# Block B's q and k for tokens 0 to 1023: seven block products for eight, in turns with plain groups

## The chip, the cores and the metric

The kernel runs on one core of one Trainium2 chip. The metric is device time in microseconds of one execution; the times are medians of several runs. The engines are named as in the profile: PE (TensorE matmul) with PEld (its weight load), DVE (VectorE), ACT (ScalarE), POOL (GpSimd) and SP (SyncE, which here issues nearly all DMAs, in the order in which they were written). Every engine works its instructions off in program order.

## What is computed

Two attention blocks on independent inputs of 2048 tokens x 640, their outputs side by side. Block A is local and dilated (8 keys, 2 apart), block B full attention; both have 32 heads of 20. All is float32.

```python
# block A: per token 8 keys, idx = pos - 2 * (0..7)
qkv = x @ wqkv ; logits = q . k[idx] * Dh**-0.5 ; o = softmax(logits) . v[idx] ; out_a = o @ wo
# block B
qkv = x @ wqkv ; p = softmax(q k^T * Dh**-0.5) ; out_b = (p v) @ wo
return concatenate([out_a, out_b], -1)
```

A float32 operand is kept as two parts, `hi` (rounded to the type that PE multiplies at full rate) and `lo = x - hi`; a product of two operands is three matmuls, hi·hi, hi·lo and lo·hi (`PASSES`). Contraction over 640 is five chunks of 128 (`KC`), so a plain output tile of 128 x 512 is 15 matmuls.

## The kernel before

The program is one long function, `attention_pair`, in four stages; nearly every instruction is issued through a recording helper, so the profile gives them one line (L61) and they are told apart by tile names.

1. Block A's q, k and v for most tokens (`a_steps`, to about 148 us). Much of it is in quads (`a_quad`): four output tiles by seven block products with sums of operands (Strassen's method in Winograd's form) in place of eight, with a fifth chunk added plainly. Results go to `qa_d`, `ka_d`, `va_d` in DRAM.
2. Block B's q and k (148 to 284 us), the stage that the change rewrites.
3. Block B's v (28 groups of 15 matmuls with 320 columns, `v_group`), and from its eighth group on the first maxima (`b_max`) of block B's scores.
4. Block B's scores, exponentials and products with v, a hand-written order of PE's work over some 1300 us, with block A's attention on POOL beside it, then the output products.

Stage 2 before is one loop (`for m in range(0, 10, 2)`): five pairs of weight blocks (`WB`, 128 q or k features each, in the order `MS`), for each four token tiles of 512 (`XB[n]`, tile names `xn` for chunks 0 to 3 and `xl` for chunk 4) and for each the two blocks: 40 groups. A group is 15 matmuls into one PSUM bank, ACT copies the high part to an output tile `pr`, DVE subtracts for the low part, and SP stores both (512 KB) to `qb_d` or `kb_d`. The output tiles come from the ring `p` of `PB` = 6 buffers. The next pair of weights is loaded through the ring `stg`, and split by ACT and DVE, two groups after the loop has reached the second token tile.

`tick()` counts groups; `after(n, fn)` places a step n ticks later, so the numbers of groups set the program order. `a_work` is the generator `a_attention`: each `next(a_work)` gives POOL one unit of block A's attention (two keys or two values of 128 tokens; tiles `akv`, with queries in `aq`), and lets SP fetch the unit after the next one (`a_fetch(n + 2)`) into a ring of 4 `akv` buffers. In stage 2 it is called after 12 of the groups 5 to 33. Four `ve` tiles, set to one by POOL before the stage, wait for stage 3 (the ones give block B's softmax sums).

In the last four groups SP also loads the keys of the first four heads (`bk`, from `kb_d`), then in stage 3 the queries (`bq`, from `qb_d`); the first maxima need both.

## Time and profile before

| | us |
|---|---|
| median of 3 runs (lowest to highest) | 1742.59 (1742.42 to 1743.18) |
| the profiled execution | 1743.04 |
| its span in the profile | 1741.3 |
| PE busy | 1728.7 (99%) |
| stage 2, first matmul to stage 3's first | 147.91 to 284.31 |
| stage 3's first maxima matmul | 300.71 |

How to read it: "busy" is the time in which an engine had an instruction at work; matmuls are pipelined, so the time that one matmul costs is read from the distance of starts and not from its duration (a row's mean of 389 ns holds two in flight). A row of a timeline gives start, duration, engine, line, operation and tiles (out<-in), a count of merged instructions, and in brackets the idle time before it with what ended it. The profile lacks some matmul records (their counts in short windows are a few per cent low). "SPq" is SP's queue; the clock column is the granted PE clock, 1.00 in every window shown.

### The profile page before, as it was taken

The page shows a single profiled execution, that of the slowest core. Times are in us where ns is not written, and L with a number is a line of the kernel's source. Part 1 is how long each engine was busy: PE and PEld are TensorE (multiplying, and loading weights), DVE is VectorE, ACT ScalarE, POOL GpSimd, SP SyncE. Part 2 cuts the span into 40 slices and gives each one's busy share as a digit, 9 for nine tenths or more (in the row PEclk, how much of TensorE's full clock was granted, in tenths as well). Part 3 has the DMA queues.
Part 4 walks back from the last instruction along what each step waited for, and adds up shares of the span by engine and source line. Part 5 has one row for each costly group of instructions (what it writes and reads, how often), then busy time and mean ns, then how long its engine had stood idle before and what let it go on. Part 6 is the DMA issues. An engine that isn't in the chain of part 4 may idle for free.

```text
span 1741.3 us, 32202 instructions
## 1 busy us (share of the span) xinstructions
PE 1728.7 (99%) x11223; PEld 981.1 (56%) x11223; DVE 1466.4 (84%) x2062; ACT 1335.5 (77%) x2603; POOL 1248.2 (72%) x1138
## 2 busy tenths in 40 slices
PE   9999999999999999999999999999999999999999
PEld 8888888874444444444444444444444444444558
DVE  7756232789999999999999999999999999999656
ACT  5224222239999999999999999999999999998882
POOL 0000991786888888887998898988888898768324
PEclk9999999999999999999999999999999999999999
DMA  7668877864546544644465455536552634231223
GB/s 236 216 215 302 289 271 239 251 194 122 165 126 145 149 132 133 168 147 139 138 171 150 133 149 142 166 104 176 147 153 91 156 100 141 67 104 47 65 74 117
DMA packets 224411, 271.20 MB, mean 156 GB/s; under 512 B 92908, under 2 KB 147448, under 8 KB 224248
## 3 DMA queue, kind: packets, MB, share of 16 engines
q1 hardware_dynamic: 223672, 268.49, 52.4%
q8 instruction: 88, 1.44, 0.4%
q14 instruction: 75, 0.61, 0.1%
q10 hardware_dynamic: 576, 0.66, 0.1%
HBM read 194.31 MB, written 74.74 MB: 155 GB/s over the span
## 4 chain that ended last, share of the span: by engine, by line
PE 94%; DVE 2%; ACT 1%; DMA 1%; issue 1%; SPq 0%; POOL 0%; DVEq 0%; POOLq 0%; ACTq 0%
PE ps_st L61 94%; DVE mx L61 2%; ACT e L61 1%; DMA bk<-kb_d 1%; DMA vb_d<-ve 0%; ACT more L61 0%; DMA qb_d<-pr 0%; DVE mtr L61 0%; SPq L61 0%; POOL am L61 0%; DVE ro L61 0%; DVE pr L61 0%; ACT al L61 0%; ACT pr L61 0%; ACT braw L61 0%
## 5 line engine op out<-in xcount | busy, mean ns | idle before, releaser
L61 DVE TENSOR_REDUCE mx<-ps_st 128x1 f32<-128x512 f32 (+1 forms) x1500 | 1217.7, 877 | 76.5 <-PE ps_st L61 65.5
L61 ACT ACTIVATE e<-ps_st 128x512 f32<-128x512 f32 x2048 | 1067.4, 609 | 45.2 <-PE ps_st L61 25.8
L61 PE MATMUL ps_st<-bq,bk 62*128 62x512 f32 x2048 | 612.8, 439 | 0.2
L61 PE MATMUL ps_st<-bk,bq 60*128 60x512 f32 x2048 | 557.5, 435 | 2.6 <-DVE mx L61 0.9
L61 PEld LDWEIGHTS ps_st<-bq,bk 62*128 62x128 f32 x2048 | 287.4, 184 | 481.0 <-ACT e L61 337.3
L61 PE MATMUL ps_st<-e,vb 128*32 128x512 f32 x4096 | 542.9, 604 | 2.1
L61 POOL TENSOR_TENSOR braw<-braw,more 128x512 f32<-128x512 f32 x224 | 287.8, 1285 | 124.4 <-ACT more L61 116.2
L61 POOL TENSOR_TENSOR akv<-akv 128x640 f32<-128x640 f32 (+3 forms) x304 | 282.2, 928 | 23.8
L61 PEld LDWEIGHTS ps_st<-bk,bq 60*128 60x128 f32 x2048 | 265.4, 184 | 35.8 <-DVE mx L61 11.9
L61 POOL TENSOR_TENSOR akv<-akv,aq 128x1280 f32<-128x1280 f32 x64 | 188.8, 2950 | 21.9 <-DMA akv<-ka_d 21.8
L61 PEld LDWEIGHTS ps_st<-e,vb 128*32 128x32 f32 x4096 | 82.0, 108 | 156.1 <-issue 70.8
L61 POOL TENSOR_TENSOR akv<-akv,al 128x1280 f32<-128x1280 f32 x64 | 152.0, 2375 | 0.2
L61 ACT COPY more<-ps_st 128x512 f32<-128x512 f32 x224 | 132.5, 591 | 1.9 <-PE ps_st L61 1.0
L61 PE MATMUL ps_st<-wc,xn 128*128 128x512 f32 (+1 forms) x544 | 133.7, 378 | 0.0
L61 ACT COPY ro<-ps_st 128x320 f32<-128x320 f32 (+2 forms) x76 | 34.8, 460 | 106.2 <-PE ps_st L61 85.1
L61 PE MATMUL ps_st<-xn,w 128*128 128x512 f32 x480 | 115.4, 389 | 0.0
L61 PEld LDWEIGHTS ps_st<-wc,xn 128*128 128x128 f32 x544 | 102.4, 188 | 14.7
L61 POOL MEMSET ve<- 128x347 f32 x4 | 1.4, 390 | 148.5 <-DVE ro L61 137.2
L61 PEld LDWEIGHTS ps_st<-xn,w 128*128 128x128 f32 x480 | 90.0, 188 | 18.9 <-issue 0.2
L61 DVE TENSOR_TENSOR pr<-ps_st,pr 128x512 fp32r<-128x512 f32 x40 | 27.6, 690 | 84.8 <-ACT pr L61 84.8
L61 ACT CAST pr<-ps_st 128x512 fp32r<-128x512 f32 x40 | 23.5, 588 | 97.2 <-PE ps_st L61 92.8
L61 PE MATMUL ps_st<-ww,aot 128*128 128x320 f32 x480 | 77.8, 314 | 1.7
(109 smaller groups left out, 1325.6 us busy)
## 6 DMA issues: line engine op xcount, KB each, us to landing
akv<-ka_d SPq DMA_DIRECT2D x128, 320.0 KB
akv<-va_d SPq DMA_DIRECT2D x128, 320.0 KB
wx<-wa_d SPq DMA_DIRECT2D x24, 480.0 KB
kb_d<-pr SPq DMA_DIRECT2D x20, 512.0 KB
qb_d<-pr SPq DMA_DIRECT2D x20, 512.0 KB
bk<-kb_d SPq DMA_DIRECT2D x16, 640.0 KB
bq<-qb_d SPq DMA_DIRECT2D x64, 160.0 KB
rb<-s_d SPq DMA_DIRECT2D x128, 64.0 KB
```

Of the source, the lines that this page charges most:

```text
L61: return self.tc.keep_in_program_order(op(*a, **k))
```

## The change

In stage 2 the eight tiles of a weight pair by four token tiles are parted. Token tiles 2 and 3 stay plain (`b_plain`: four groups of 15). Token tiles 0 and 1 with the pair's two weight blocks become a four (`b_four`): the weight blocks' even and odd chunks are A11, A12 (first block) and A21, A22 (second), the token tiles' are B11, B21 and B12, B22; sums S1 to S4 of the former and T1 to T4 of the latter make seven products of 2 chunks x 3 passes, and the fifth chunk is added to each of the four results. A four is parted at four places (30, 6, 15 and 3 matmuls), and each counts as a group. The turns are: plain 0, plain 1, four 0, four 1, plain 2, four 2, plain 3, four 3, four 4, plain 4.

- The token sums (`XFour`, tiles `xs`, `xn`) are made once, by POOL on the raw tiles after groups 2 and 4; their parts by ACT and DVE (`base`, `second`). The weight sums (`WFour`) are made on POOL for pairs 0 and 1 and on DVE for pairs 2 to 4, and parted likewise. `jobs` says after which group each stands; pair 1's weights are loaded after group 0.
- Partial results are summed by DVE (tiles `sum` in the rings `raw` and `rb`). The low part of an output and its store stand one group later (`low`).
- The ring `p` of 6 becomes two rings `px` and `p` of 3, taken in turns elsewhere; in stage 2 all outputs use the 3 of `p` and `px` holds parts of the tokens. The ring `akv` becomes `akv` and `akx` of 2 each; in stage 2 (`narrow`) the attention units have only the 2 of `akv`, their first fetches stand at groups 7 and 9, and the fetch of unit n + 2 stands three groups after unit n. The units stand at groups 9 to 33, again 12.
- The `ve` tiles are set to one at the end of the stage. Large tiles change places (`big` 0 and 1 with 2 and 3), since the plain tiles are now 2 and 3; `ident` moves into the ring `am`.

```diff
+    def p_tile(shape, dt=F32R, name="wc", tag=None):
+
+        if tag is None:
+            turn_p[0] += 1
+            tag = ("px", "p")[turn_p[0] % 2]
+        return sb.tile(shape, dt, tag=tag, bufs=PB // 2, name=name)
...
-        kv = sb.tile([128, 2, D], F32, tag="akv", bufs=4, name="akv")
+        turn_kv[0] += not narrow[0]
+        kv = sb.tile([128, 2, D], F32, tag=("akv", "akx")[turn_kv[0] % 2], bufs=2, name="akv")
...
-            a_fetch(n + 2)
+            if not narrow[0]:
+                a_fetch(n + 2)
...
+            if narrow[0]:
+                after(3, a_fetch, n + 2)
...
+        def sums(self, kp):
+            a, b = self.raw[kp]
+            pool(b[:, 1], b[:, 1], b[:, 0], ALU.subtract)
+            pool(b[:, 0], b[:, 0], a[:, 0], ALU.subtract)
+            pool(a[:, 0], b[:, 1], a[:, 0], ALU.add)
+            pool(a[:, 1], a[:, 1], a[:, 0], ALU.subtract)
+
+        def second(self, kp):
+            u, e = self.u[1][:, :, 2 * kp:2 * kp + 2], self.e[kp]
+            self.parts(u[:, 0], u[:, 1], self.raw[kp][0])
+            for n in range(2):
+                self.parts(e[n + 1][:, 0], e[n + 1][:, 1], self.raw[kp][1][:, n])
...
-    groups = 0
-    for m in range(0, 10, 2):
-        nxt = []
-        for n in range(4):
-            for j in range(2):
-                p = next(banks)
-                for k in range(KC):
-                    for i, (wi, xi) in enumerate(PASSES):
-                        pe.matmul(p, WB[j][:, wi, k], chunk(XB[n], xi, k), start=(k == 0 and i == 0),
-                                  stop=(k == KC - 1 and i == 2))
...
-                pt = sb.tile([128, 2, 512], F32R, tag="p", bufs=PB, name="pr")
-                act.copy(pt[:, o[0]], p)
-                dve.tensor_tensor(pt[:, o[1]], p, pt[:, o[0]].bitcast(F32), ALU.subtract)
-                after(1, sp.dma_start, dst_b(c, n).rearrange("t p c -> p t c"), pt.bitcast(F32))
-                tick()
...
+    def b_parts(p, c, n, first=None, wait=False):
+
+        o = (0, 1) if c < KC else (1, 0)
+        pt = p_tile([128, 2, 512], F32R, "pr", "p")
+        src = p
+        if first is not None:
+            src = pt[:, o[1]].bitcast(F32)
+            add(src, first, p)
+        if wait:
+            lows.append(lambda: act.copy(pt[:, o[0]], src))
+        else:
+            act.copy(pt[:, o[0]], src)
+
+        def lo():
+            lo_of(pt[:, o[1]], src, pt[:, o[0]])
+            sp.dma_start(dst_b(c, n).rearrange("t p c -> p t c"), pt.bitcast(F32))
+        lows.append(lo)
...
+        product(b[0], A11, B11, True, True)
+        act.copy(c[0], b[0])
+        low()
+        product(b[3], w.S(4) + v1, B22 + l2, True, True)
+        product(b[1], w.S(2), x.T(2), True, True)
+        add(c[1], c[0], b[1])
+        product(b[0], A12 + v1, B21 + l1, False, True)
+        b_parts(b[0], m[0], 0)
+        yield
+        product(b[2], w.S(1), x.T(1), True, True)
+        add(c[1], c[1], b[2])
+        low()
+        b_parts(b[3], m[0], 1, c[1])
+        yield
+        product(b[1], w.S(3), x.T(3), False, True)
+        add(c[0], c[0], b[1])
+        low()
+        product(b[4], A22 + v2, x.T(4) + l1, True, True)
+        b_parts(b[4], m[1], 0, c[0])
+        yield
+        product(b[2], v2, l2, False, True)
+        b_parts(b[2], m[1], 1, c[0], True)
+        low(2)
+        yield
...
+    jobs = {0: (kp1, lambda: WF.append(WFour(1, "stg", 3))), 1: (lambda: XW.base(0),),
+            2: (lambda: XW.sums(0), lambda: WF[1].base()), 3: (lambda: WF[0].sums(gp), lambda: XW.ends([ends_x[1][:, o] for o in range(2)])),
+            4: (lambda: XW.second(0), lambda: XW.base(1), lambda: XW.sums(1)), 5: (lambda: WF[0].second(), lambda: WF[1].sums(gp)),
+            6: (lambda: XW.second(1),), 7: (lambda: a_fetch(0),), 8: (lambda: WF[1].second(),), 9: (lambda: a_fetch(1),)}
+    for m, at in ((2, (10, 13, 16, 18)), (3, (18, 21, 24, 25)), (4, (25, 27, 28, 29))):
...
+        if groups in (9, 11, 14, 16, 18, 21, 23, 25, 27, 29, 31, 33):
+            next(a_work, None)
```

How this moves the instructions is seen on three engines. On PE, where plain groups of before become the fourth four (`xn`, `xl`, `xs`: token tiles; `w`: weights):

```order
-L61 MATMUL ps_st<-xn,w 128x512 x12
+L61 MATMUL ps_st<-xn,w 128x512 x6
+L61 MATMUL ps_st<-xs,w 128x512 x6
 L61 MATMUL ps_st<-xl,w 128x512 x3
 L61 MATMUL ps_st<-xn,w 128x512 x12
 L61 MATMUL ps_st<-xl,w 128x512 x3
-L61 MATMUL ps_st<-xn,w 128x512 x12
+L61 MATMUL ps_st<-xs,w 128x512 x12
+L61 MATMUL ps_st<-xn,w 128x512 x6
+L61 MATMUL ps_st<-xl,w 128x512 x6
```

The rows with + or a blank are one four: 6 + 6 + 3 + 12 + 3 + 12 + 6 + 6 = 54 matmuls, where four plain groups have 60.

On POOL, at the start of its work in stage 2, before (`ve`: the tiles set to one; `akv`: the first attention unit):

```order
L61 MEMSET zero 7x128
L61 MEMSET ve 128x347 x4
L61 TENSOR_TENSOR akv<-akv,aq 128x1280
L61 TENSOR_TENSOR akv<-akv 128x2x320
L61 TENSOR_TENSOR akv<-akv 128x2x160
```

and now (`stg`: raw tokens, 512 wide, and raw weights, 2x128):

```order
L61 MEMSET zero 7x128
L61 TENSOR_TENSOR stg<-stg 128x512 x4
L61 TENSOR_TENSOR stg<-stg 128x2x128 x4
L61 TENSOR_TENSOR stg<-stg 128x512 x4
L61 TENSOR_TENSOR stg<-stg 128x2x128 x4
L61 TENSOR_TENSOR akv<-akv,aq 128x1280
```

Sixteen sums stand ahead of the first unit, and the four settings have gone behind the last one.

On SP's queue, at the end of stage 2, before (`pr`: outputs; `wv_b`: weights of stage 3; `bk`: keys for the maxima):

```order
L61 DMA stg<-wv_b 128x320
L61 DMA bk<-kb_d 40x4x1024
L61 DMA qb_d<-pr 128x2x512
L61 DMA bk<-kb_d 22x4x1024
L61 DMA qb_d<-pr 128x2x512
L61 DMA stg<-wv_b 128x640 x2
L61 DMA stg<-wv_b 128x320
L61 DMA bk<-kb_d 40x4x1024
L61 DMA qb_d<-pr 128x2x512
L61 DMA bk<-kb_d 22x4x1024
L61 DMA vb_d<-ve 128x336
```

and now (`akv`: the fetch of an attention unit's keys):

```order
L61 DMA akv<-ka_d 128x640 x2
L61 DMA stg<-wv_b 128x320
L61 DMA bk<-kb_d 40x4x1024
L61 DMA qb_d<-pr 128x2x512
L61 DMA bk<-kb_d 22x4x1024
L61 DMA qb_d<-pr 128x2x512
L61 DMA stg<-wv_b 128x640 x2
L61 DMA stg<-wv_b 128x320
L61 DMA bk<-kb_d 40x4x1024
L61 DMA qb_d<-pr 128x2x512
L61 DMA bk<-kb_d 22x4x1024
L61 DMA qb_d<-pr 128x2x512
```

A key fetch has come in ahead of the key loads, and each `bk` load now stands one store earlier: the last of them ahead of the last group's store, which `vb_d<-ve` follows.

More of the change, by code (lines that the diff above doesn't have):

```diff
@@ L299, in __init__ @@
                 w = [sb.tile([128, 3, n], F32R, tag="w", bufs=4, name="wc") for _ in range(4)]
-                p = [sb.tile([128, 2, n], F32R, tag="p", bufs=PB, name="wc") for _ in range(PB)]
+                p = [p_tile([128, 2, n]) for _ in range(PB)]
                 self.b11 = [[w[2 * kp + i][:, 2] for i in range(2)] for kp in range(2)]
@@ L313, in __init__ @@
             self.c = [[lambda i, j=j: self.last[j][i]] for j in range(2)]
-            self.raw = [sb.tile([128, 2, n], F32, tag=tag, bufs=2 * (P + 1), name="wr") for tag, _ in self.tags for _ in range(2)]
+            self.raw = [sb.tile([128, 2, n], F32, tag=tag, bufs=2, name="wr") for tag, _ in self.tags for _ in range(2)]
             self.raw.append(end)
@@ L700, in x_raw @@
+    XW, WF = XFour(), []
     def x_raw(n, a, b, tag, bufs):
@@ L834, in attention_pair @@
[L834 removed]
+                t = 3 - o if n == 44 else o
+                sp.dma_start(r[:, o], xb[(KC - 1) * 128:, t * 512:(t + 1) * 512])
+            ends_x.append(r)
         if n == 45:
[L836 to L840 removed]
+            WF[0].base()
         elif n == 46:
[L842 removed]
@@ L843, in attention_pair @@
-            x_parts(0, KC - 1, ends_x[0])
+            XB[3][1] = sb.tile([128, 2, 1, 512], F32R, tag="last1", bufs=2, name="xl")
+            x_parts(3, KC - 1, ends_x[0][:, :1])
         if n in (45, 46):
-            raw_x += [x_raw(n - 43, a, b, "p", PB) for a, b in PAIRS[:2]]
-    XB.append(columns(1))
-    x_parts(1, 0, raw_x[0])
-    x_parts(1, 2, raw_x[1])
-    x_parts(1, KC - 1, ends_x[1])
+            a, b = PAIRS[n - 45]
+            r = p_tile([128, b - a, 512], F32, "stg", "p")
+            sp.dma_start(r, xb[a * 128:b * 128, 1024:1536].rearrange("(k p) c -> p k c", p=128))
@@ L850, in attention_pair @@
+            raw_x.append(r)
+    XB[2] = columns(2)
+    x_parts(2, 0, raw_x[2])
+    x_parts(2, 2, raw_x[3])
+    x_parts(2, KC - 1, ends_x[0][:, 1:])
     assert not keeps
-    ones = [sb.tile([128, 16 * VC + 11], F32, tag=tag, bufs=2, name="ve") for tag in ("raw", "rb", "raw", "rb")]
-    for t in ones:
-        gp.memset(t, 1.0)
     wait[0] = 2
@@ new lines, in b_four @@
+    def b_four(w, x):
+        A11, A12, A22 = ([w.block(j, 2 * kp + o) for kp in range(2)] for j, o in ((0, 0), (0, 1), (1, 1)))
+        B11, B21, B22 = ([f(kp) for kp in range(2)] for f in (x.B11, x.B21, x.B22))
+        v1, v2 = ([w.block(j, KC - 1)] for j in range(2))
+        l1, l2 = ([t] for t in x.l)
+        m = w.m
+        b = [next_bank() for _ in range(5)]
+        c = [sb.tile([128, 512], F32, tag=tag, bufs=2, name="sum") for tag in ("raw", "rb")]
+        product(b[0], A11, B11, True, True)
[22 more added lines that the diff above has]
+        yield
@@ new lines, in b_plain, with groups_b @@
+    def b_plain(w):
+        for n in (3, 2):
+            for j in range(2):
+                p = next_bank()
+                product(p, [w.block(j, k) for k in range(KC)],
+                        [lambda i, k=k: chunk(XB[n], i, k) for k in range(KC)], True, True)
+                low()
+                b_parts(p, w.m[j], n)
+                yield
+    def groups_b():
+        for kind, m in ((0, 0), (0, 1), (1, 0), (1, 1), (0, 2), (1, 2), (0, 3), (1, 3), (1, 4), (0, 4)):
+            yield from b_four(WF[m], XW) if kind else b_plain(WF[m])
@@ new lines, in attention_pair @@
+    for m, at in ((2, (10, 13, 16, 18)), (3, (18, 21, 24, 25)), (4, (25, 27, 28, 29))):
+        for g, fn in zip(at, (lambda m=m: WF.append(WFour(m, "stg", 3)), lambda m=m: WF[m].base(),
+                              lambda m=m: WF[m].sums(dve), lambda m=m: WF[m].second())):
+            jobs[g] = (*jobs.get(g, ()), fn)
+    for groups, _ in enumerate(groups_b()):
+        tick()
+        for fn in jobs.get(groups, ()):
+            fn()
+        if loads:
+            loads.pop(0)()
+        if groups == 33:
+            WV, loads = wide_pieces(wv_b[0])
+        elif groups == 38:
+            wait[0] = 4
+            w1, more = wide_pieces(wv_b[1])
+            for fn in more:
+                fn()
+        if groups > 35:
+            if groups == 36:
+                k_loads = b_keys(0)
+                rings.append(big(1, [128, NQC, 2, 512], "bq"))
+                q_loads = [fn for qc in range(NQC) for fn in b_queries(0, qc)]
+            k_loads.pop(0)()
+        if groups in (9, 11, 14, 16, 18, 21, 23, 25, 27, 29, 31, 33):
+            next(a_work, None)
@@ L936, in attention_pair @@
+    low()
     tick()
+    narrow[0] = False
+    ones = [sb.tile([128, 16 * VC + 11], F32, tag=tag, bufs=2, name="ve") for tag in ("raw", "rb", "raw", "rb")]
+    for t in ones:
+        gp.memset(t, 1.0)
     def max_rows(m4, m1, q, qc):
```

153 lines of the change are left out of this document (92 added, 61 removed).

## Prediction

> **What bounds the kernel now.** I read the page first: which engine is full, and which carries the chain that ended last.
>
> ```profile
> span 1741.3 us, 32202 instructions
> PE 1728.7 (99%) x11223; PEld 981.1 (56%) x11223; DVE 1466.4 (84%) x2062; ACT 1335.5 (77%) x2603; POOL 1248.2 (72%) x1138
> ...
> PE 94%; DVE 2%; ACT 1%; DMA 1%; issue 1%; SPq 0%; POOL 0%; DVEq 0%; POOLq 0%; ACTq 0%
> ```
>
> TensorE is never at rest, but a busy PE alone does not say that every matmul counts; so next the stretch that the change rewrites, block B's q and k, as windows (columns: stretch, length, busy us of PE, PEld, DVE, ACT, POOL with counts, clock, DMA share, GB/s):
>
> ```profile
> 148.30:165.00 16.70, 16.70 (x74) 13.48 (x73) 12.07 (x15) 10.12 (x14) 0.71 (x2) 1.00 0.80 300
> 165.00:185.00 20.00, 20.00 (x90) 16.56 (x89) 6.52 (x10) 4.78 (x8) 10.43 (x8) 1.00 0.96 343
> 185.00:205.00 20.00, 20.00 (x90) 16.54 (x89) 5.87 (x8) 4.78 (x8) 18.82 (x19) 1.00 0.86 294
> 265.00:284.30 19.30, 19.30 (x86) 15.96 (x86) 5.79 (x9) 4.55 (x8) 1.29 (x4) 1.00 0.77 247
> ```
>
> PE has no idle in it, DVE and ACT are two thirds free from 165 on, POOL is nearly full in the middle, and the DMA queue is the one other thing near its end. Last, PE's timeline at both ends of the stretch, and the groups:
>
> ```profile
> 147.91 2.95 PE L61 MATMUL ps_st<-xn,w 128*128 128x512 f32 x12
> ...
> 151.66 2.93 PE L61 MATMUL ps_st<-xn,w 128*128 128x512 f32 x12
> ...
> 155.11 2.88 PE L61 MATMUL ps_st<-xn,w 128*128 128x512 f32 x12
> ...
> 158.51 2.88 PE L61 MATMUL ps_st<-xn,w 128*128 128x512 f32 x12
> ```
> ```profile
> 284.31 1.92 PE L61 MATMUL ps_st<-ww,xn 128*128 128x320 f32 x12
> ```
> ```profile
> L61 PE MATMUL ps_st<-xn,w 128*128 128x512 f32 x480 | 115.4, 389 | 0.0
> L61 PE MATMUL ps_st<-xl,w 128*128 128x512 f32 x120 | 34.0, 390 | 0.0
> ```
>
> 600 matmuls in 40 groups of 15. A group starts 3.40 us after the one before it (155.11 to 158.51), so a matmul costs 3.40 / 15 = 0.2267 us, and counted back from 155.11 group 0 stands at 148.3; 40 groups are 136.0 of the 136.4 us from 147.91 to 284.31, and the other 0.35 is a late first group (3.75 instead of 3.40). So here a matmul less is 0.2267 us less, as long as operands come in time.
>
> **Part 1, the products.** A four does four output tiles with 7 block products of 6 matmuls and 4 times 3 for the fifth chunk: 54 instead of 60. Five fours save 30 matmuls: 30 x 0.2267 = 6.80 us. Does a matmul in a four cost the same? The quads of block A already have this form, with sums on DVE between products:
>
> ```profile
> 132.21 0.61 PE L61 MATMUL ps_st<-wc,xn 128*128 128x512 f32 x2
> ...
> 134.93 0.61 PE L61 MATMUL ps_st<-wc,xn 128*128 128x512 f32 x2
> ```
>
> Four times 3 matmuls lie between these two rows: 2.72 / 12 = 0.2267 us. Same price.
>
> **Part 2, the work beside it.** By these rows:
>
> ```profile
> 129.76 0.69 DVE L61 TENSOR_TENSOR sum<-sum,ps_st 128x512 f32<-128x512 f32 x1 [2.18 <-PE ps_st L61]
> ```
> ```profile
> L61 DVE TENSOR_TENSOR xn<-stg,xn 128x1024 fp32r<-128x1024 f32 x6 | 7.2, 1220 | 0.8 <-ACT xn L61 0.5 <-DMA kb_d<-pr 0.3
> L61 DVE TENSOR_TENSOR pr<-ps_st,pr 128x512 fp32r<-128x512 f32 x9 | 6.2, 690 | 11.6 <-ACT pr L61 11.6
> L61 DVE TENSOR_TENSOR xl<-stg,xl 128x512 fp32r<-128x512 f32 x4 | 2.7, 684 | 1.9 <-ACT xl L61 1.9
> ```
> ```profile
> L61 ACT CAST xn<-stg 128x1024 fp32r<-128x1024 f32 x6 | 6.2, 1053 | 0.0
> L61 ACT CAST pr<-ps_st 128x512 fp32r<-128x512 f32 x9 | 5.3, 588 | 15.7 <-PE ps_st L61 11.3 <-DVE xl L61 1.8 <-DVE xn L61 1.3
> ```
> ```profile
> L61 POOL TENSOR_TENSOR xl<-stg,xl 128x512 fp32r<-128x512 f32 x1 | 1.3, 1286 | 0.0
> L61 POOL TENSOR_TENSOR al<-al,am 128x256 f32<-128x256 f32 x4 | 3.0, 740 | 0.5 <-DVE am L61 0.5
> ```
>
> A four gives DVE 6 adds and 4 low parts, 10 x 0.69 = 6.9 us of its 54 x 0.2267 = 12.24, its weights' low parts (2304 columns at 0.684 per 512) and sums some 5 us, and the four plain groups beside it 4 x 0.69 = 2.8: 14.7 of the 25.8 us that a four and a plain block last, under 60% of DVE. Nothing there reaches PE, except where a deadline is short. There are two such places.
>
> **The first four (start 148.3 + 8 x 3.40 = 175.5).** POOL makes the token sums: 2 x 4 adds of 512 and, for two weight pairs, 2 x 4 of 256: 8 x 1.286 + 8 x 0.740 = 16.2 us, before its first attention unit. The second four adds wait for DVE's low part of the raw tiles. Group 4 ends at 165.5, then ACT casts 0.5, 0.95, 0.5, 0.5, 0.95, 0.5 and DVE follows: about 171.3. POOL: 171.3 + 4 x 1.286 = 176.4. ACT then casts the new sums (0.95 + 0.5 + 0.5) and, queued behind, the eighth group's tile and the first product's copy (0.5 each): 179.4. The third block product that accumulates on that bank may not begin before; PE gets there 21 matmuls into the four, 175.5 + 4.76 = 180.3. So 0.9 us to spare. But POOL beside DVE is slower:
>
> ```profile
> 190.93 3.46 POOL L61 TENSOR_TENSOR akv<-akv 128x640 f32<-128x640 f32 x4
> ...
> 197.78 4.52 POOL L61 TENSOR_TENSOR akv<-akv 128x640 f32<-128x640 f32 x4
> ```
> ```profile
> 196.73 0.69 DVE L61 TENSOR_TENSOR pr<-ps_st,pr 128x512 fp32r<-128x512 f32 x1 [2.71 <-ACT pr L61]
> 197.35 1.02 DVE L61 TENSOR_TENSOR w<-stg,w 128x640 fp32r<-128x640 f32 x1
> ```
>
> The same four adds took 4.52 instead of 3.46 us while DVE made a weight's low part of 640 columns: 1.06 more. In 171.3 to 176.4 DVE makes three of them, 1024 columns: 1.06 x 1024 / 640 = 1.7 us, if all of it collides. Then PE waits 1.7 - 0.9 = 0.8. I take 0.4, between none and 0.8. The Trainium skill (SBUF — State Buffer, "Who interferes with whom") says that a VectorE instruction with two SBUF inputs and a GpSimd instruction that reads SBUF take one shared port as an exclusive lock, for a whole instruction. By that rule PE would wait 0.4 us here (POOL blocked for three low parts of about 1.3 us together); the trace's 1.06 agrees in kind and is a little dearer.
>
> **Weights just in time.** The second pair's weights are loaded only after group 0 and used at group 4 (161.9); those of pairs 2 and 3 are cast after the four's second part, 4.1 us before use. Cast and low part end about 0.9 us ahead for the one, 0 to 0.2 ahead for the two others. I take 0.2 us for all; 2.0 if the DMA queue, 0.96 busy at 165 to 185, brings the first of them late.
>
> **Outputs and keys.** Three output buffers instead of six: a store must have landed three groups (10.2 us) later. Two key buffers instead of four: the fetch of unit n+2 stands on SP until POOL is done with unit n, and the stores of the next groups stand behind it.
>
> ```profile
> 187.91 2.95 POOL L61 TENSOR_TENSOR akv<-akv,aq 128x1280 f32<-128x1280 f32 x1
> ...
> 194.75 2.95 POOL L61 TENSOR_TENSOR akv<-akv,aq 128x1280 f32<-128x1280 f32 x1
> ```
>
> A unit takes POOL 6.84 us; 12 units are given out over groups 9 to 33, one per 6.9 us. POOL just keeps up, SP waits 0 to 2 us at a fetch, and the store ring holds 10.2: 0 on PE.
>
> **The end of the stretch.** Its loads decide when the maxima can begin:
>
> ```profile
> 279.04 3.28 DMA qb_d<-pr
> ...
> 284.75 10.85 DMA bk<-kb_d
> ...
> 295.66 6.02 DMA vb_d<-ve
> ```
> ```profile
> 300.71 0.46 PE L61 MATMUL ps_st<-bk,bq 60*128 60x512 f32 x1 [0.84 <-DMA bq<-qb_d]
> 301.74 0.70 PE L61 MATMUL ps_st<-bk,bq 60*128 60x512 f32 x3 [0.57 <-DMA vb_d<-ve]
> ```
> ```profile
> 285.84 0.38 SPq L61 DMA_DIRECT2D qb_d<-pr  x1
> 286.26 0.42 SPq L61 DMA_DIRECT2D bk<-kb_d  x1
> ```
>
> PE waits 0.84 + 0.57 = 1.4 us. The chain starts at a group's output, so it moves with PE. Now each key load stands ahead of the store of its group instead of behind it (up to 3.4 us earlier for the last), but a key fetch of 640 KB more stands in front (1.9 us at the 343 GB/s of the row at 165). Between all of the wait gone (-1.4) and 1.9 more I take -0.3: the fetch comes some 8 us before the end, into a queue that is 0.77 busy, and is mostly absorbed there.
>
> **The sum.** -6.80 + 0.4 + 0.2 - 0.3 = -6.5 us. The profiled execution took 1743.04 us, its span of 1741.3 and 1.7 around it; less 6.5 is 1736.5. It lay 0.45 above the median of the runs, 1742.59: 1736.1.
>
> **The rivals.** *The first four starves* (slip of weights and POOL together): 2.0 for the weights, 0.8 for POOL and 1.0 for later pairs take back 3.8 of the 6.5: 1739.8. For it: margins under 1 us and the DMA share of 0.96. Against: a late PE gives the others time, so slips do not add up in full. 0.13.
>
> *The gain reappears as a wait at the maxima*: if the DMA engines and not PE pace the end (0.77 busy), the first maxima still begin at 301.7 and the time stays 1742.6. Against: the chain above leads back to PE's group. 0.08.
>
> *Slower: POOL holds SP.* If each of the 12 units waits out its fetch, because the store queue delays it (3.28 us for one DMA, the row above), a unit costs 6.84 + 3.28 = 10.1. The first fetch stands behind the seventh store (about 180.5) and lands near 184, so the last unit ends at 184 + 12 x 10.1 = 305 instead of 184 + 12 x 6.84 = 266. SP would hold the last stores and the key loads until then. The ring covers 10.2 us; the other 29 fall on PE: 1736 + 29 = 1765; with half of the fetches exposed, 1736 + 9 = 1745. It decides once POOL runs more than 10.2 + 6.5 us late. Against: of the two buffers one is always loaded while POOL works 6.84 us on the other. 0.05.
>
> *The change does not do what it says*: the matmuls are not fewer or not as cheap. The order shows 54 for a four and the quads cost the same. 0.03, at 1742.6.
>
> **How the numbers follow.** The forecast has the rest, 0.71; its own range is 1734.4 (all of 6.8 and 1.4) to 1738.7 (0.8 for POOL, 0.2 for weights, 1.9 at the end). A measurement of this kernel can tell 0.2%, 3.5 us: faster is below 1739.1. That holds the forecast and about half of the first rival: 0.71 + 0.07 = 0.78; the same 0.06 + 0.08 + 0.03 = 0.17; slower 0.05. A range from 1734.4 to 1739.9 takes in the forecast and the first rival, 0.84 together, of which their own tails take a little: eight in ten.
>
> **What would show it.** Right: 570 matmuls in the stretch, 129.6 us or less from its first to block B's v (136.4 before), plain groups still 3.40 apart, PE idle under 1 us before the third product of the first four, about 1 us at the first maxima. Wrong: idle on PE behind ACT or POOL at about 180; SP waiting on POOL for several us with ACT or DVE then waiting for a store; the first maxima still near 301.

## The result and the profile after

The kernel after takes 1764.05 us (median of 4 runs, 1761.55 to 1766.12) beside 1742.51 for the kernel before: a ratio of 1.0123 [1.0105, 1.0140]. It is slower by some 21 us where 6.5 faster was forecast. The page of the kernel after:

```profile
span 1762.4 us, 32277 instructions
PE 1733.5 (98%) x11193; PEld 980.1 (56%) x11193; DVE 1534.7 (87%) x2130; ACT 1347.7 (76%) x2634; POOL 1273.3 (72%) x1154
...
PE 77%; DVE 2%; ACT 2%; DMA 2%; POOL 1%; issue 1%; SPq 0%; DVEq 0%; POOLq 0%; ACTq 0%
```

The 30 matmuls are gone (11193 for 11223), and yet the span is 21.1 us longer. The last row is the chain that ended last. Its 77% for PE can't be set against the 94% before: this chain can be followed back to 272.43 us only, the one before to the start of the span. The windows of stage 2 (columns as in the prediction) show where the time goes. Two of the kernel before, then four of the kernel after:

```profile
205.00:225.00 20.00, 20.00 (x90) 16.57 (x89) 5.06 (x8) 4.15 (x7) 18.82 (x20) 1.00 0.73 255
...
245.00:265.00 20.00, 20.00 (x90) 16.57 (x89) 7.32 (x10) 4.78 (x8) 19.51 (x13) 1.00 0.79 278
```

```profile
165.00:185.00 20.00, 19.22 (x83) 15.18 (x82) 18.33 (x19) 10.77 (x19) 15.34 (x13) 1.00 0.28 106
...
205.00:225.00 20.00, 19.53 (x86) 15.83 (x85) 18.27 (x20) 5.18 (x10) 18.76 (x19) 1.00 0.70 234
...
245.00:265.00 20.00, 14.08 (x50) 10.57 (x49) 13.93 (x19) 5.80 (x12) 15.17 (x16) 0.83 0.79 274
265.00:284.00 19.00, 16.23 (x64) 12.65 (x63) 15.01 (x22) 4.59 (x9) 10.17 (x6) 0.91 0.53 189
```

DVE, 25 to 37% full in these windows before, is over 90% full in the first two; PE loses 6 us in the third, and there its clock falls to 0.83. PE's timeline names the waits (the number in brackets is the idle time, with what ended it):

```profile
182.38 2.15 PE L61 MATMUL ps_st<-xn,w 128*128 128x512 f32 x7 [0.78 <-DVE xn L61]
...
248.49 0.50 PE L61 MATMUL ps_st<-xs,w 128*128 128x512 f32 x1 [1.63 <-ACT w L61]
...
256.75 2.93 PE L61 MATMUL ps_st<-xn,w 128*128 128x512 f32 x6 [4.07 <-ACT sum L61]
...
268.68 1.65 PE L61 MATMUL ps_st<-xl,w 128*128 128x512 f32 x3 [2.54 <-DVE sum L61]
...
300.92 0.94 PE L61 MATMUL ps_st<-ww,xl 128*128 128x320 f32 x3 [1.63 <-ACT ww L61]
...
320.61 0.77 PE L61 MATMUL ps_st<-bk,bq 60*128 60x512 f32 x1 [4.02 <-DMA bq<-qb_d]
```

Stage 2 runs from 147.66 to 297.38: 149.7 us, 13.3 more than before. From there to the V group behind the first maxima (322.81) it is 25.4 us where it was 18.1 (284.31 to 302.37): 7.4 more. These two are 20.7 of the 21.1 us. For its 570 matmuls stage 2 would need 570 x 0.2267 = 129.2 us, so it is 20.5 too long: 11.7 are PE's waits (6.8 for a four's sums, 3.8 for weights, 1.1 for token parts), and the other 8.8 are rows that run slower, most of them behind waits: six matmuls that take 1.52 us elsewhere took 2.93 behind the wait of 4.07. Of the 7.4 at the end, 2.9 are longer waits at the first maxima (4.3 for 1.4), 1.6 the wait at 300.92 for weights of stage 3 (`ww`), and the rest slower rows.

Why is DVE so full? Its groups by form in the kernel after, 180 to 300 (columns: count, busy us, mean ns):

```profile
L61 DVE TENSOR_TENSOR pr<-pr 128x512 fp32r<-128x512 f32 x15 | 23.4, 1579 | 1.0 <-ACT pr L61 0.3
L61 DVE TENSOR_TENSOR stg<-stg 128x256 f32<-128x256 f32 x12 | 12.1, 1008 | 0.3
L61 DVE TENSOR_TENSOR pr<-ps_st,pr 128x512 fp32r<-128x512 f32 x17 | 11.2, 676 | 0.0
L61 DVE TENSOR_TENSOR w<-stg,w 128x512 fp32r<-128x512 f32 x7 | 10.7, 1526 | 1.8 <-ACT w L61 1.7
```

One subtraction of 512 columns takes 676 ns when one input is in PSUM (`ps_st`) and 1579 or 1526 when both are in SBUF. The timelines of DVE and POOL, side by side, show what the long ones stand beside:

```profile
209.19 4.29 DVE L61 TENSOR_TENSOR pr<-pr 128x512 fp32r<-128x512 f32 x2
```
```profile
208.00 2.95 POOL L61 TENSOR_TENSOR akv<-akv,aq 128x1280 f32<-128x1280 f32 x1
211.02 4.25 POOL L61 TENSOR_TENSOR akv<-akv 128x640 f32<-128x640 f32 x4
```

Two low parts, 1.4 us by themselves, last 4.29. Taken singly in the trace, the first ends at 211.50, 0.55 us after POOL's product (210.95), and the second at 213.47, 0.55 after POOL's first add (212.93): each stands until an instruction of POOL has ended.

How does a late DVE hold PE? By the order of the queues, as the two longest waits show. First ACT's and then DVE's timeline:

```profile
252.56 0.58 ACT L61 CAST pr<-ps_st 128x512 fp32r<-128x512 f32 x1 [3.02 <-DMA qb_d<-pr]
254.30 1.62 ACT L61 CAST w<-stg 128x640 fp32r<-128x640 f32 x3 [1.15 <-DMA stg<-wqk_b]
255.82 0.41 ACT L61 ACTIVATE al<-al 128x256 f32<-128x256 f32 x1
256.14 0.56 ACT L61 COPY sum<-ps_st 128x512 f32<-128x512 f32 x1
```
```profile
260.88 7.15 DVE L61 TENSOR_TENSOR stg<-stg 128x256 f32<-128x256 f32 x4
267.95 0.67 DVE L61 TENSOR_TENSOR sum<-sum,ps_st 128x512 f32<-128x512 f32 x1
```

The copy at 256.14 ends PE's wait of 4.07. Ahead of it ACT stood 3.02 us for a free output buffer (a store that had not landed), then 1.15 for the load of the next pair's weights, and then cast these. The sum at 267.95 ends the wait of 2.54. Ahead of it stand four sums of the next pair's weights with two SBUF inputs: 7.15 us, where four without POOL's long work take 4 x 0.497 = 2.0 (the kernel with light units, below).

At the end of the stage, the chain of the kernel after runs through a unit on POOL, then through SP (which waits 1.3 us for POOL before a key fetch), a store and the loads:

```profile
286.03 2.34 POOL akv L61
...
294.22 9.74 DMA qb_d<-pr
...
303.98 13.52 DMA bk<-kb_d
...
317.52 4.09 DMA bq<-qb_d
```

### The profile page after: what moved, and what is told of

Same layout as the page of the kernel before. It is cut to its first block, busy times and chain, and to the rows that moved or that the text cites. A ratio compares the mean times of both kernels' runs of the same rounds, so it can differ in the third digit from the quotient of the medians.

```text
span 1762.4 us, 32277 instructions
## 1 busy us (share of the span) xinstructions
PE 1733.5 (98%) x11193; PEld 980.1 (56%) x11193; DVE 1534.7 (87%) x2130; ACT 1347.7 (76%) x2634; POOL 1273.3 (72%) x1154
## 4 chain that ended last, share of the span: by engine, by line
PE 77%; DVE 2%; ACT 2%; DMA 2%; POOL 1%; issue 1%; SPq 0%; DVEq 0%; POOLq 0%; ACTq 0%
PE ps_st L61 77%; DVE mx L61 2%; ACT e L61 1%; DMA bk<-kb_d 1%; DMA qb_d<-pr 1%; POOL akv L61 0%; ACT more L61 0%; DMA akv<-va_d 0%; DMA bq<-qb_d 0%; POOL ao L61 0%; SPq L61 0%; DVE mtr L61 0%; POOL am L61 0%; DVE ro L61 0%; DVE am L61 0%
## 5 line engine op out<-in xcount | busy, mean ns | idle before, releaser
L61 ACT ACTIVATE e<-ps_st 128x512 f32<-128x512 f32 x2048 | 1067.3, 609 | 45.3 <-PE ps_st L61 23.6
L61 POOL TENSOR_TENSOR akv<-akv 128x640 f32<-128x640 f32 (+3 forms) x304 | 286.2, 941 | 23.8
L61 POOL TENSOR_TENSOR stg<-stg 128x512 f32<-128x512 f32 (+1 forms) x16 | 20.3, 1273 | 161.4 <-DVE xs L61 157.5
L61 PE MATMUL ps_st<-xn,w 128*128 128x512 f32 x360 | 92.3, 400 | 6.9 <-ACT sum L61 4.3
L61 PEld LDWEIGHTS ps_st<-xn,w 128*128 128x128 f32 x360 | 68.4, 192 | 25.3 <-ACT sum L61 6.0
L61 DVE TENSOR_TENSOR sum<-sum,ps_st 128x512 f32<-128x512 f32 (+2 forms) x69 | 41.1, 596 | 46.0 <-PE ps_st L61 40.2
L61 POOL TENSOR_TENSOR ao<-ao,akv 128x640 f32<-128x640 f32 x48 | 75.5, 1573 | 3.8
```

The source lines that it names most:

```text
L61: return self.tc.keep_in_program_order(op(*a, **k))
```

## The experiments

Four theories were weighed. *Port*: DVE's instructions with two SBUF inputs and POOL's instructions shut each other out. *Rings*: the smaller rings hold SP. *Queue*: what stands late in ACT's and DVE's program order ahead of a four's sums holds PE. *End*: the late transfers crowd. Ratios are to the kernel before, run beside each kernel on the same chip.

**Last sums of a four in their bank.** The sum is written in place in PSUM; the low part of the output then has one SBUF input. Nothing else changes.

```diff
-            src = pt[:, o[1]].bitcast(F32)
-            add(src, first, p)
+            add(p, first, p)
```

> The adds that finish an output of a four are written back into the PSUM bank, so that the 15 low parts that read two SBUF tiles (pr<-pr, 1579 ns each in the changed kernel) read one SBUF tile and one bank (690 ns). Nothing else changes. Port theory (a DVE instruction with two SBUF inputs waits out whole POOL instructions, and the lateness of DVE is what reaches PE through SP's queue): DVE gets 15 x 0.9 = 13 us back in the stretch and the time falls by 5 to 15 us, to 1749 to 1759. Ring theory (three output and two key buffers behind SP's in-order queue would stall anyway): within 2 us of 1764.

Measured 1.0083 [1.0068, 1.0098], 7 us better than after and inside the port theory's range. DVE's groups:

```profile
L61 DVE TENSOR_TENSOR pr<-ps_st,pr 128x512 fp32r<-128x512 f32 x34 | 22.8, 683 | 10.3 <-ACT pr L61 9.8
L61 DVE TENSOR_TENSOR stg<-stg 128x256 f32<-128x256 f32 x12 | 15.2, 1265 | 0.3
```

The same 15 low parts fall from 1579 to 683 ns by the place of one input; the forms that keep two SBUF inputs stay long. The same work, read from elsewhere, gives back a third of the loss, and the intervals do not touch. This is the clearest sign for the port.

**The rings alone.** The kernel before with the smaller rings and the change's places for units and fetches, but all products plain.

```diff
+        turn_kv[0] += not narrow[0]
+        kv = sb.tile([128, 2, D], F32, tag=("akv", "akx")[turn_kv[0] % 2], bufs=2, name="akv")
...
+                pt = p_tile([128, 2, 512], F32R, "pr", "p")
```

> The kernel before, with the small rings alone: outputs of block B's q and k in three buffers, attention units in two, fetched at the places of the changed kernel, 12 units at its groups; no fours. Port theory: DVE has 8 such instructions in the stretch as before, so 1741 to 1746. Ring theory: a good part of the 21 us, 1752 to 1765.

Measured 1.0006 [0.9996, 1.0015]. Its window:

```profile
245.00:265.00 20.00, 20.00 (x90) 16.57 (x89) 8.46 (x10) 4.78 (x8) 18.81 (x13) 1.00 0.82 288
```

PE is never idle beside a POOL that is fuller than after (18.81 for 15.17 us). So neither the rings nor POOL's units cost anything by themselves; they need the fours. The reverse was not run: no kernel has the fours with six output buffers.

**Light units.** The products and the long sums of the 12 units in stage 2 are left out on POOL (block A's first 256 tokens are not formed).

```diff
+        if not light:
             pool(kv, kv, q.unsqueeze(1).to_broadcast([128, 2, D]), ALU.mult)
```

> The changed kernel, where the 12 attention units of block B's q and k leave out their products and long sums on POOL (a key unit keeps only its last 64-wide add, a value unit only the adds into its result), so block A's result for the first 256 tokens is not formed. Fetches and their order stay. Port theory: DVE's instructions go back to 690 ns, the stretch to about 131 us and the time to 1736 to 1741. Ring theory: also faster, since POOL frees its buffers at once, but DVE's durations would have nothing to do with POOL and pr<-pr would stay near 1579 ns.

Measured 1.0019 [1.0008, 1.0030]: 18 of the 21 us are gone, though the gain that the port theory expected did not appear. DVE's groups and the first maxima:

```profile
L61 DVE TENSOR_TENSOR pr<-pr 128x512 fp32r<-128x512 f32 x15 | 10.5, 712 | 1.2 <-ACT pr L61 0.3
L61 DVE TENSOR_TENSOR stg<-stg 128x256 f32<-128x256 f32 x12 | 6.0, 497 | 0.3
L61 DVE TENSOR_TENSOR w<-stg,w 128x512 fp32r<-128x512 f32 x7 | 4.8, 690 | 3.6 <-ACT w L61 3.6
```
```profile
303.70 0.47 PE L61 MATMUL ps_st<-bk,bq 60*128 60x512 f32 x1 [3.68 <-DMA bq<-qb_d]
```

Against the kernel after, these three forms need (1579 - 712) x 15 + (1008 - 497) x 12 + (1526 - 690) x 7 = 25 us less of DVE. Stage 2 ends at 281.71, 2.6 before the kernel before; but the first maxima begin at 303.70 and give it back. So POOL's long work beside the fours is most of the loss, and there is something at the end that is not POOL's long work.

**No fetches.** Units 2 to 11 work on the first two key tiles again in place of their own keys and values, so SP neither fetches for them nor waits for POOL.

```diff
+        if narrow[0] and 1 < n < 12:
+            a_kv[n] = a_old[n % 2]
+            return
```

> The changed kernel, where units 2 to 11 work on the two key tiles that were fetched first: POOL does the same arithmetic, but SP neither waits for POOL nor moves 6.6 MB of keys and values in the stretch (block A's result for the first 256 tokens is not right for that). Ring theory: SP is free, the outputs' stores are prompt, 1736 to 1745. Port theory: DVE still waits for POOL, pr<-pr stays over 1200 ns; some time is won by the missing wait and transfers, but more than half of the 21 us stays: 1753 to 1762.

Measured 1.0093 [1.0078, 1.0109]. Most of the loss stays without these ten fetches, and `pr<-pr` stays at 1234 ns: the rival of the prediction, POOL holding SP, is not the main way. Its share is at most the 5 us that this kernel is better, with intervals that touch, and half of that is at the end (22.8 us for 25.4): the wait for `bq` fell from 4.3 to 0.4, but 2.0 for `vb_d` came in its place.

**Two edits together, and weights by way of a bank.** In the first, the sums of the weights of pairs 2 to 4 go to POOL as well as the last sums into the bank; in the second, ACT also copies the weights' high parts to an eighth bank, from which DVE reads.

```diff
-                              lambda m=m: WF[m].sums(dve), lambda m=m: WF[m].second())):
+                              lambda m=m: WF[m].sums(gp), lambda m=m: WF[m].second())):
```

> The kernel after with two edits: the last sums of a four of products are added in place in their PSUM bank, and the sums of the weights of pairs 2 to 4 are formed by POOL instead of DVE. Left on DVE with two inputs in SBUF: only the low parts of weights and tokens. Port theory (each such DVE instruction waits for a whole POOL instruction and POOL for it): the twelve stg<-stg sums, 12.1 us of DVE, go; the low parts of the weights stay stretched, at 1200 to 1600 ns for 512 columns against 690 without units; PE's waits for sums go, those for weights stay in part; ratio to before 1.003 to 1.008. Startup theory (the rest of the loss comes from the outputs' stores that stand behind the first sums on DVE and so on SP's queue): the DMA share stays near 0.28 in 165 to 185, the first unit is fetched near 185 as after. Rival (POOL is the bound, and more work on it makes it later): ratio above 1.010.

```diff
+                act.copy(s, u[:, 0, a:a + n].bitcast(F32))
+                dve.tensor_tensor(u[:, 1, a:a + n], raw[:, a:a + n], s, ALU.subtract)
```

> As the one before, and the weights' high parts are also copied by ACT to an eighth PSUM bank, which DVE reads for the low parts; products and plain groups take turns over the other seven banks. Then DVE has no instruction with two inputs in SBUF while units run, apart from the tokens' parts at the start of the stage. Port theory: low parts of 512 columns near 690 ns, no PE wait for DVE's w, sum or pr above 0.5 us after 185, stage 2 from 147.7 to 281 to 285; the late DMAs stay, as in the kernel with light units, so 1.001 to 1.005 of before. Rival (ACT's extra copies or seven banks instead of eight hold PE): waits for ACT's w or for banks, ratio above 1.007.

Measured 1.0133 [1.0118, 1.0148] and 1.0109 [1.0094, 1.0125]: the port theory missed both, and both lie where the rivals had them. In the second DVE's forms for products and weights are at their short times (687 ns for 512 columns), and yet PE's waits in stage 2 sum to 14.5 us (11.7 after). The second kernel's ACT and POOL timelines tell why:

```profile
249.30 0.62 ACT L61 CAST w<-stg 128x512 fp32r<-128x512 f32 x1 [5.61 <-POOL stg L61]
```
```profile
242.29 3.46 POOL L61 TENSOR_TENSOR akv<-akv 128x640 f32<-128x640 f32 x4
...
246.11 3.16 POOL L61 TENSOR_TENSOR stg<-stg 128x256 f32<-128x256 f32 x4
```

The weights' sums now stand behind a unit in POOL's own queue, and ACT stands 5.61 us for them. These two kernels took one wait away and put another in, so they speak neither for the port nor against it.

**Low parts of the first outputs ahead of the jobs**, alone and with the edits above.

```diff
+        if groups < 8:
+            low()
         tick()
```

> The kernel after with one edit: while the first eight groups of the plain kind run, the low part of an output that has been formed is issued to DVE ahead of the jobs (parts and sums of tokens and weights) and not behind them. Startup theory: SP's seven stores of 27.7 us go earlier, the DMA share in 165 to 185 rises from 0.28 to 0.5 or more, the first unit's fetch moves from 185.7 to 165 to 178, and the late DMAs before the first maxima shrink: 3 to 6 us less than after, ratio 1.0085 to 1.0105. Port theory alone: DVE is stretched as before, and earlier units are stretched earlier; ratio 1.011 to 1.014.

> The edits of the three kernels before it together: no two SBUF inputs on DVE while units run, and the outputs' low parts ahead of the first jobs. If port and startup together are the cause, nothing is left of the loss and the 30 matmuls fewer show: 6.8 us less in stage 2, first maxima at 294 to 300, ratio 0.996 to 1.000. If a third cause is left (the token parts at the start, or stores and loads crowded at the end), ratio 1.001 to 1.005 with its wait named at the first maxima.

Measured 1.0148 [1.0133, 1.0163] and 1.0140 [1.0123, 1.0157], both above the 1.0123 of after, with intervals that touch its own. The waits of PE in the first:

```profile
PE ps_st L61 <- ACT w L61: 7.8, 2, 6.1
```

The output's store moved ahead of the second pair's weights in SP's queue, and PE stood 6.1 us for those weights, from about 162 to 168. The DMA share from 165 to 185 did rise, from 0.28 to 0.43, and no time was won. The startup theory is not borne out; what earlier stores would be worth without that wait is not shown.

**One SBUF input, nothing moved to POOL; late fetches.** The sums of pairs 2 to 4 too read one input from the eighth bank, on DVE. The second kernel leaves the units light instead and puts the fetches for units 12 and 13 behind the loads of keys and queries; the third has both edits and does all the work.

```diff
+            act.copy(s, b[0])
+            act.copy(t, a[0])
+            dve.tensor_tensor(b[1], b[1], s, ALU.add)
+            dve.tensor_tensor(b[0], t, b[0], ALU.subtract)
```

> No DVE instruction of the products or weights has two inputs in SBUF, and none of their work is moved to POOL, so that the weights of a later four cannot queue behind a unit there: last sums of a four in place in the bank, high parts and two raw blocks copied by ACT to an eighth bank, low parts and the sums of pairs 2 to 4 on DVE with one input from that bank. POOL's units are as in the kernel after. Port theory: w of 512 near 690 ns, the sums of 256 near 420, no PE wait for DVE's or ACT's w and sum above 0.6 us after 200, stage 2 ends at 281 to 284, and what is left is the wait for bq at the first maxima: ratio 1.000 to 1.004, as with light units. Rival (it is POOL's units by themselves, not the port: moved to POOL or not, the PE waits stay): ratio 1.007 to 1.012.

```diff
-                after(3, a_fetch, n + 2)
+                after(3 if n < 10 else 13, a_fetch, n + 2)
```

> The kernel with light units (as before, products and long sums of 12 units left out, A's first 256 tokens not formed) with one more edit: the fetches for units 12 and 13 are put into stage 3, behind the loads of keys and queries. Backlog theory (stage 2 is shorter and its transfers later, so that the last stores, these fetches and the loads of keys crowd): the DMA share in 265 to 284 falls from 1.01 to 0.85 to 0.95, the last load of keys lands 2 to 4 us earlier, PE's wait for bq falls from 4.0 to 0.5 to 2, ratio 0.9990 to 1.0007 against 1.0019. Rival (the chain of the last store and the loads behind it has its length by itself): ratio 1.0015 to 1.0025.

> Both edits together, all work done: one SBUF input on DVE, and the fetches for units 12 and 13 in stage 3. If port and backlog are the causes and add: 0.998 to 1.002 of before. If the units on POOL hold the rest by themselves: 1.006 or more.

Measured 1.0081 [1.0064, 1.0097], 1.0003 [0.9993, 1.0012] and 1.0052 [1.0037, 1.0067]. Late fetches are worth 3 us with light units and 5 with full ones, though in both pairs the intervals touch. With full units they bring the time from stage 3's start to the V group behind the first maxima from 22.4 to 18.0 us, as long as before. With light units the time came as the backlog theory said, but the wait for `bq` only fell from 4.0 to 3.8. The first kernel is a miss by the port theory's numbers: no gain over the sums in the bank alone. PE's long waits in the third kernel:

```profile
253.76 2.93 PE L61 MATMUL ps_st<-xn,w 128*128 128x512 f32 x6 [3.08 <-ACT sum L61]
...
268.21 1.63 PE L61 MATMUL ps_st<-xs,w 128*128 128x512 f32 x6 [2.57 <-DVE sum L61]
```

The first stands at the same product as after, the second two products later, at the start of the next four, with DVE about half empty (9.68 of 20 and 11.88 of 19 us busy in the windows from 245 and from 265).

**Where the preparation stands; the end.** The first kernel moves the jobs of pairs 3 and 4 beside plain groups and those of pair 2 a little earlier. The second has late fetches and issues the low parts of the last plain four at once. The third has both and the last sums in the bank. The fourth is the second with light units.

```diff
-    for m, at in ((2, (10, 13, 16, 18)), (3, (18, 21, 24, 25)), (4, (25, 27, 28, 29))):
+    for m, at in ((2, (9, 12, 14, 15)), (3, (15, 17, 18, 19)), (4, (19, 24, 25, 26))):
```

> The kernel after with one edit: the jobs that prepare the weights of pairs 3 and 4 (load, base parts, sums, second parts) are issued at groups 15, 17, 18, 19 and 19, 24, 25, 26 instead of 18, 21, 24, 25 and 25, 27, 28, 29, so that all of it stands beside plain groups and none in front of a running four's sums; pair 2 one to four groups earlier. POOL's units and DVE's two SBUF inputs stay. Queue theory (the stretched preparation stands ahead of a four's own sums in ACT's and DVE's queues): PE's waits for ACT's sum (4.3) and DVE's sum (2.5) fall under 1 us in total and the granted clock stays at 0.97 or more from 245 to 284, DVE's instructions stay as long as in the kernel after (pr<-pr 1300 to 1600 ns); ratio 1.004 to 1.009. Rival (DVE as a whole is too full when stretched, wherever the work stands): the waits move to another four, ratio 1.010 to 1.013.

```diff
                 b_parts(p, w.m[j], n)
+                if w.m[1] == MS[-1]:
+                    low()
                 yield
```

> The kernel after with two edits at the end of the stretch: the fetches for units 12 and 13 in stage 3, behind the loads of keys and queries, and the low parts of the last plain four issued to DVE at once and not a group later. Tail theory: the last store leaves SP within 2 us of stage 2's end (5.8 us with light units), PE's wait for bq falls from 4.3 to under 1.5, first maxima within 18 us of the start of stage 3 (23.2 after, 16.4 before); ratio 1.007 to 1.010. Rival (loads of keys have their 10 to 13 us whatever is in front): ratio 1.011 to 1.013.

> All work done: weights' preparation beside plain groups, both edits at the end of the stretch, and the last sums of a four in place in the bank. If queue and tail are the causes and add up: ratio 0.996 to 1.001, stage 2 ends at 278 to 282. If DVE's load under POOL's units sets it: 1.004 or more.

> Light units (products and long sums of 12 units left out, A's first 256 tokens not formed), late fetches, and the last low parts issued at once. Tail theory: last store of a query at 282 to 284 against 286.96, wait for bq 3.8 falls under 1, ratio 0.996 to 0.9985, which is the prediction's time, since without POOL's long instructions nothing else is left. Rival: 1.000 as with the late fetches alone.

Measured 1.0108 [1.0093, 1.0123], 1.0101 [1.0084, 1.0118], 1.0078 [1.0063, 1.0093] and 1.0002 [0.9992, 1.0011]. The first went as its rival said; PE's timeline:

```profile
206.72 1.65 PE L61 MATMUL ps_st<-xl,w 128*128 128x512 f32 x3 [3.83 <-DVE sum L61]
...
229.98 2.44 PE L61 MATMUL ps_st<-xn,w 128*128 128x512 f32 x6 [2.35 <-ACT sum L61]
...
263.71 2.12 PE L61 MATMUL ps_st<-xs,w 128*128 128x512 f32 x6 [2.58 <-DVE sum L61]
```

Two of the waits are at other fours now, and in stage 2 they sum to 10.3 us (11.7 after). In this kernel where the stretched work stands decides which four waits, and little of how much. The end theory held in part in the second: the wait for `bq` fell to 2.0 (under 1.5 expected), the time to 1.0101, and the interval touches that of after. The third, with all work done, came as its second theory said, and its end is 18.0 us, as before. The fourth came as its rival said; with light units the end still is not as short as before:

```profile
282.44 1.92 PE L61 MATMUL ps_st<-ww,xn 128*128 128x320 f32 x12
...
301.27 0.47 PE L61 MATMUL ps_st<-bk,bq 60*128 60x512 f32 x1 [1.72 <-DMA bq<-qb_d]
302.55 0.95 PE L61 MATMUL ps_st<-bk,bq 60*128 60x512 f32 x3 [0.81 <-DMA bq<-qb_d]
```

From stage 3's start to the V group at 303.43 it is 21.0 us, where it was 18.1. Stage 2 ends 1.9 us earlier than before, but the first maxima do not begin earlier: 301.27 here, 300.87 with late fetches alone, 300.71 before.

**No softmax steps.** ACT and DVE also work off an exponential, a maximum and a reciprocal for each tile of block A, whose inputs POOL makes. These kernels leave them out in stage 2 (a row of POOL's takes the maximum's place, the mask is left out; block A's first 256 tokens are formed without softmax): on the kernel after, on the one with a single SBUF input and both edits at the end, and on the one with all three moves.

```diff
+        if not narrow[0]:
+            act.activation(L, L, AF.Exp, scale=SCALE)
```

> The kernel after, with the softmax steps of the first two tiles' units in stage 2 left out of DVE's and ACT's queues (one maximum of 32, one exponential, one reciprocal each, and the mask; POOL takes a row in place of the maximum; A's first 256 tokens are not formed rightly); all of POOL's long products and sums stay. Port theory (DVE's instructions with two SBUF inputs are what POOL stretches, and the softmax steps are no more than 2 of the 21 us): ratio 1.010 to 1.013, pr<-pr still 1300 to 1600 ns. Rival (ACT and DVE stand at softmax steps that wait for POOL, with a four's sums behind): the waits for ACT's sum and DVE's sum of 6.8 us go, granted clock 0.97 or more in 245 to 284, ratio 1.003 to 1.008.

> One SBUF input for all products and weights, late fetches, last low parts at once, and no softmax steps in stage 2 (as above). With the port taken away and the softmax steps too, POOL's long work has no way left to hold PE: if these two are the ways, ratio 0.998 to 1.002 as with light units. If PE's waits for sums stay (then it is the copies that ACT and DVE hand each other over the one bank): 1.003 to 1.006.

> Preparation beside plain groups, end of stretch, last sums in the bank (1.0078 together), and no softmax steps in stage 2. Port theory: the wait of 4.5 at 208 (behind weights stretched to 5.1 us) stays, the one of 3.6 at 264 (behind a reciprocal that waits 1.7 for POOL) shrinks by 1.5 to 3: ratio 1.005 to 1.007. Rival: both go, 1.001 to 1.004.

Measured 1.0097 [1.0081, 1.0114], 1.0043 [1.0026, 1.0061] and 1.0065 [1.0050, 1.0080]. The first is 4.5 us under the kernel after, more than the port theory allowed and less than its rival did; since the intervals touch, it is a sign and no proof. The third came inside the port theory's range, with the wait of 4.5 still 4.1. In the second, with one SBUF input and no softmax steps, PE still waits, and the time is in the range given for the hand-over of the bank. Its PE and DVE timelines:

```profile
264.89 1.61 PE L61 MATMUL ps_st<-xs,w 128*128 128x512 f32 x6 [2.96 <-DVE sum L61]
```
```profile
261.62 0.69 DVE L61 TENSOR_TENSOR w<-stg,ps_st 128x512 fp32r<-128x512 f32 x1 [1.80 <-ACT ps_st L61]
262.81 0.42 DVE L61 TENSOR_TENSOR w<-stg,ps_st 128x256 fp32r<-128x256 f32 x1 [0.50 <-ACT ps_st L61]
263.72 0.42 DVE L61 TENSOR_TENSOR w<-stg,ps_st 128x256 fp32r<-128x256 f32 x1 [0.50 <-ACT ps_st L61]
264.06 0.68 DVE L61 TENSOR_TENSOR sum<-sum,ps_st 128x512 f32<-128x512 f32 x1
```

The sum that PE waits for stands in DVE's queue behind three low parts, and each of these waits for a copy of ACT's to the one bank. So the remedy has a price of its own here: the two engines hand each other that bank, and from 180 to 300 DVE stands 27 us for such copies. That is a likely reason why the single SBUF input gave no more than the sums in the bank alone; a kernel with two such banks was not run.

No kernel with all the work beats the kernel before; the nearest is at 1.0052.

## Why the prediction was wrong, point by point

**The products: right.** 30 matmuls fewer are in the page. The price held too: with light units and both edits at the end, the last plain groups, at which PE does not wait, start 3.40 us apart (272.24, 275.64, 279.04).

**"Under 60% of DVE. Nothing there reaches PE": the step that failed.** The instructions were counted well, and priced by rows taken while POOL was idle or DVE alone. 34 of them from 180 on (the three forms above) have two SBUF inputs, and POOL's long instructions run beside most of them: 25 us more of DVE, 18.27 of 20 us busy in one window where at most 12 were forecast. PE's waits for sums in stage 2, put at nothing, were 6.8 us, and with the other waits and the slower rows the stage is 20.5 over its 129.2. The prediction had the collision in hand, the row of four POOL adds at 4.52 instead of 3.46 us and the Trainium skill (SBUF — State Buffer, "Who interferes with whom"), which has a DVE instruction with two SBUF inputs and a GpSimd instruction that reads SBUF take the shared port as an exclusive lock for a whole instruction. By that rule the forms with one input in PSUM stay short, and the trace agrees: 676 against 1579 ns. The prediction used row and rule in one direction, POOL delayed by short DVE instructions, and at one place, the first four. The other direction costs more here: DVE waits out an instruction of POOL, and one product of 1280 columns lasts 2.95 us.

How it reaches PE is a second part of the same step. A busy share under 100% was taken for cover. But a four's sums stand in program order behind the preparation of a later pair, and PE needs each sum within a product or two. The four sums of 7.15 us ahead of one sum are such a case, and so are the output buffer and the weights for which ACT stood ahead of its copy. A queue that is late by 3 us at that point costs 3 us, however empty it is on the average: the kernel with DVE half empty waited at one of the same places and close to the other. The runs put POOL's long work beside the fours, by all ways together, at 18 of the 21 us (1.0123 to 1.0019). Where 15 of DVE's instructions read one input is 7 of these. How the others split between DVE's stretched preparation, outputs that wait for a buffer, softmax steps that wait for POOL (a sign of 4.5) and the fetches at the end (3 to 5) was not settled: the edits overlap, and their gains do not add up.

**The first four and the weights just in time: right in kind, too small.** At the first four 0.78 came for a forecast of 0.4. For weights PE waited 3.8 us in the whole stage for a forecast of 0.2: 0.67 at the fifth group, the rest at later pairs, 1.63 of it at 248.49. In the first kernel with light units only the 0.67 is left, which puts the rest down to the step above.

**"Outputs and keys: 0 on PE": right alone, wrong beside the fours.** The rings alone cost nothing (1.0006). With the fours, SP waits 6.5 us for POOL from 148 to 298, and ACT stands 23.6 us from 185 to 298 for an output buffer whose store has not landed; in the kernel before and with the rings alone it never does. That is one of the prediction's own signs of being wrong. How much of the loss six buffers would save is open.

**The end of the stretch: wrong sign.** -0.3 was forecast for the wait at the maxima, +2.9 came; with the weights of stage 3 and the slower rows the end is 7.4 longer. That a key fetch is mostly absorbed there did not hold: where the two last fetches were moved behind the loads, with one SBUF input and all the work, the end was 18.0 us again.

**The rivals.** "POOL holds SP" gave a time in the range that came, by a mechanism that the kernel without fetches shows to be minor: that the time fits is luck. "The gain reappears as a wait at the maxima" is what is left where POOL's long work is out: stage 2 ends earlier, the first maxima begin near 301, and the time is that of the kernel before (1.0002 and 1.0003). With light units and both edits the chain from 274.30 to 302.41 is nearly all loads (7.87 and 9.84 us for weights, 9.36 for queries), and the DMA share from 265 to 284 is 0.94 (0.77 before). That fits this rival; no run tests it further. None of the rivals had DVE as the engine that becomes late, and that is why they left 0.05 for slower.

**What is left.** With light units and the end mended the ratio is 1.0002, not 0.9963. Of these 6.8 us, 2.5 are PE's waits up to 205, for weights above all, and 2.9 are the end; most of the rest is slower rows in stage 2 (134.5 us less 129.2 and the 2.5 of waits: 2.8). So even without POOL's long work beside it this form of the change did not gain what its matmuls save.

## What to carry to other kernels

Price an instruction in the company it will have: a DVE instruction with two SBUF inputs and 512 columns took 1579 ns beside POOL's long instructions and 712 without them, and one input in PSUM brought it back to 683. When work moves to an engine, read in the program order what will stand ahead of the results that the bounding engine waits for; a mean load says nothing of that. The same goes for a free buffer: a late result holds the store, the store holds the buffer, and the buffer holds the next result. And a remedy that hands data through one more engine or one more bank is to be counted as a wait of its own.

## What the runs showed of the hardware

Behind PE's waits the granted clock fell, which the prediction had not counted. Windows of the kernel after, to the end of its longest wait and behind it:

```profile
245.00:256.70 11.70, 5.83 (x24) 3.94 (x22) 7.49 (x13) 5.22 (x11) 8.04 (x7) 0.92 0.96 328
256.70:265.00 8.30, 8.25 (x26) 6.62 (x27) 6.44 (x7) 0.58 (x1) 7.14 (x9) 0.70 0.56 197
```

The clock is 0.70 in the 8.3 us in which PE works again without a pause, so a wait of 4 us costs more than its 4 us: against 0.2267 us a matmul, the 21 matmuls from 256.75 to 263.93 took 2.4 us too long, and the nine from 268.68 to 272.35, behind the wait of 2.54, 1.6. It is no fixed rule here: behind a wait of 2.96 us in the kernel with one SBUF input and no softmax steps six matmuls took 1.61 us, at a clock of 1.00 in the window.
